# Attention taps by way of a DRAM buffer, bands by a masked multiply, and the combine in source order

## The chip, the cores and the metric

The kernel runs on one core of a Trainium2 chip. The metric is the device time of one execution in microseconds (us), taken over several runs. A profiled execution of the kernel before the change gives the views that are quoted below.

## The reference

First a short convolution whose weights differ per token and head: 8 batches of 3584 tokens with 192 features, 8 heads of 24 features, 7 taps. The taps of each token and head are softmaxed. Then a soft mixture of experts over all 28672 tokens with 32 slots and 8 experts.

```python
w = exp(weight_gen - max over taps); w = w / (sum over taps + 1e-09)
out[b, s, h*24:(h+1)*24] = sum over k of w[b, s, h, k] * x_pad[b, s + k, h*24:(h+1)*24]   # x_pad: 6 zero rows in front
logits = out @ phi                                   # 28672 x 32
d = softmax of logits over the tokens;  slot_input = d.T @ out
slot_out[e] = relu(slot_input[e] @ w1[e]) @ w2[e]
result = (softmax of logits over the slots) @ slot_out
```

## The kernel before

**Tiling.** A block is 26 tokens (`T`). Four blocks make a group of 104 tokens, and there are 35 groups in a batch, 280 in all. TensorE works on two groups at a time, a *pair*, so there are 140 pairs. Eight pairs make a *unit* `u`. Seven groups, which are 3.5 pairs, make a *supergroup* `s`; there are 40 of them, and x and the taps are loaded by supergroup.

**The convolution as a matrix product.** For each block, and each half of the heads, a weight matrix is needed that has 4 bands on its partitions: 32 input rows for each of 4 heads, and 26 columns for the block's tokens. Column j holds the 7 taps of token j at rows j to j+6 and zero elsewhere. `conv` multiplies it with a block-diagonal tile of x (`xbd`, two buffers) into one of three PSUM tiles (`cvs`), and ScalarE copies the result to `tms`. A supergroup has 56 such bands (`NBC`).

**How a band is made before.** The host lays the taps out by token with 8 slots (`KS`), tap k of token j at slot (j+k) mod 8. `loadw` brings one supergroup. `taps_top` (VectorE) finds the maximum, `taps_exp` subtracts it (VectorE) and takes the exponential (ScalarE), `taps_sum` sums and inverts (VectorE), `taps_norm` multiplies (GpSimd). `bandw` then makes half a supergroup's bands: `band_mult` (GpSimd) repeats the 8 slots four times and multiplies by the band mask, with tokens on partitions, and `band_turn` (VectorE) transposes 32x32 blocks so that the input rows come onto the partitions.

**What follows.** `xpose` transposes `tms` on TensorE and ScalarE copies it to `cms`. Once per unit: `logits` (TensorE, then maximum `mx` and `mq` on VectorE), `dexp` (the matmul `pm`, then an exponential), `dturn` and `save` (VectorE transposes), `dispatch` (TensorE) and `rescale` (VectorE). `soft_step` walks through the softmax over slots, half a batch at a time, on VectorE, GpSimd and ScalarE. After the last unit come the experts, and then the combine: for each piece of the output `rows` multiplies on TensorE, `leave` copies from PSUM on ScalarE and VectorE in turn and sends the piece to DRAM, and `turn` (VectorE) transposes the softmaxed logits of a later batch into `cT`.

**What sets the order.** A planner with its own estimate of times orders the instructions of PE, DVE, ACT and POOL, except inside blocks that are marked `manual_schedule`, where program order holds: the start (DVE, POOL, ACT) and the stretch from the last unit to the end of the experts (all four). SP, which issues every DMA, always follows program order: an issue that waits holds up all that stand behind it. `loadx(s)` waits until `conv` has finished with supergroup s-2. In the loop, `loadw(s+3)` stands at the start of supergroup s, behind `loadx(s+1)`.

## Time and profile before

| what | value |
|---|---|
| median of 3 runs | 400.87 us (398.52 to 402.51) |
| profiled execution | 401.48 us, of which the span of its instructions is 399.8 us |
| busy share of the span | PE 80%, DVE 78%, POOL 64%, ACT 47% |
| DMA | 72.69 MB, mean 182 GB/s |
| mean granted TensorE clock | 0.897 of full |

Shares are of the whole span, which has stages with different limits: a start of some 22 us, the loop over units until about 310 us, the experts until 331 us, and the combine, in which the output is written. An engine's busy time includes time in which an instruction has begun and is held by another engine. "DVE idle before, released by DMA" means that an instruction of VectorE waited for a transfer.

### The profile page before, as it was taken

The numbers are of one execution on the slowest core, as the hardware profiler recorded it, in microseconds if no ns is written. First come the engines' busy times: TensorE is split into PE (matmuls) and PEld (weight loads), VectorE is DVE, ScalarE is ACT, GpSimd is POOL, SyncE is SP. The second block draws the span as 40 slices with busy tenths as digits, with TensorE's granted clock in tenths as the row PEclk, the third lists the DMA queues.
The fourth block names the chain that finished last, engine by engine and source line by source line (L and its number), as shares of the span: only waits on it lengthen the run. The fifth ranks groups of instructions, "written<-read, shape, count | busy, mean of one in ns | idle before, by whom it ended". The sixth has DMA issues, their size and how long they took to land.

```text
span 399.8 us, 15122 instructions
## 1 busy us (share of the span) xinstructions
PE 318.3 (80%) x6624; PEld 225.8 (56%) x6624; DVE 313.8 (78%) x494; ACT 189.4 (47%) x409; POOL 257.1 (64%) x203
## 2 busy tenths in 40 slices
PE   7867777869788797986978889875889894999940
PEld 7656556647466685764757676664667651323310
DVE  8999697896899979998888978899695559654430
ACT  7555453546365564554545446563555112443320
POOL 7887777977689899598967797798694430000000
PEclk9999998998999989989897989999899999595555
DMA  6554965864763643646433375543447901999996
GB/s 179 153 142 118 271 199 150 236 203 143 212 178 96 167 114 93 168 117 158 107 106 99 95 176 132 131 119 93 117 117 285 349 5 48 362 397 399 399 402 235
DMA packets 22866, 72.69 MB, mean 182 GB/s; under 512 B 4241, under 2 KB 9489, under 8 KB 22289
## 3 DMA queue, kind: packets, MB, share of 16 engines
q1 hardware_dynamic: 22800, 71.73, 58.5%
q8 instruction: 52, 0.85, 1.0%
q14 instruction: 14, 0.11, 0.1%
HBM read 49.35 MB, written 22.36 MB: 179 GB/s over the span
## 4 chain that ended last, share of the span: by engine, by line
DVE 40%; PE 21%; DMA 18%; SPq 11%; issue 4%; ACT 2%; POOL 1%; ACTq 0%; DVEq 0%; POOLq 0%
DMA wbuf<-wh 16%; DVE wbuf L231 12%; PE cv L255 8%; SPq L651 6%; DVE en L198 5%; SPq L183 5%; DVE wmx L193 4%; DVE wsm L205 3%; DVE mq L300 3%; PE pt L268 3%; PE po L642 3%; DVE wsm L206 2%; DMA out<-big 2%; DVE mx L298 2%; DVE sm L76 1%
## 5 line engine op out<-in xcount | busy, mean ns | idle before, releaser
L215 POOL TENSOR_TENSOR wbuf<-en,mask 128x896 f32<-128x896 f32 (+1 forms) x83 | 170.6, 2076 | 5.5 <-DVE en L211 3.0
L255 PE MATMUL cv<-big,wbuf 128*26 128x96 f32 x4480 | 139.0, 259 | 31.2 <-DVE wbuf L231 20.3
L255 PEld LDWEIGHTS cv<-big,wbuf 128*26 128x26 f32 x4480 | 107.8, 110 | 53.7 <-DVE wbuf L231 27.3
L258 ACT COPY tm<-cv 128x384 f32<-128x384 f32 x140 | 65.9, 481 | 62.8 <-PE cv L255 57.8
L231 DVE STREAM_TRANSPOSE wbuf<-wbuf 128x896 f32<-128x896 f32 (+1 forms) x84 | 87.3, 1043 | 1.7 <-POOL wbuf L215 1.6
L268 PE MATMUL pt<-ident,tm 122*128 122x122 f32 x420 | 75.3, 296 | 6.5 <-ACT tm L258 5.8
L270 ACT COPY cm<-pt 128x312 f32<-128x312 f32 x139 | 56.9, 422 | 31.1 <-PE pt L268 30.4
L211 POOL TENSOR_TENSOR en<-en,wsm 128x448 f32<-128x448 f32 (+1 forms) x38 | 36.8, 967 | 40.8 <-DVE wsm L206 27.3
L268 PEld LDWEIGHTS pt<-ident,tm 122*128 122x128 f32 x420 | 46.1, 148 | 28.4 <-ACT tm L258 8.7
L642 PE MATMUL po<-cT,so 32*128 32x468 f32 (+3 forms) x256 | 47.4, 853 | 6.4 <-DVE big L649 5.4
L193 DVE TENSOR_REDUCE wmx<-wbuf 128x56 f32<-128x448 f32 (+1 forms) x41 | 24.0, 587 | 26.2 <-DMA wbuf<-wh 26.2
L649 DVE COPY big<-po 128x936 f32<-128x936 f32 (+1 forms) x24 | 26.2, 1102 | 22.0 <-DMA out<-big 11.7
L198 DVE TENSOR_TENSOR en<-wbuf,wmx 128x448 f32<-128x448 f32 (+1 forms) x40 | 43.1, 1078 | 0.1
L649 ACT COPY big<-po 128x936 f32<-128x936 f32 (+1 forms) x24 | 21.9, 918 | 39.1 <-PE po L642 20.1
L200 ACT ACTIVATE en<-en 128x448 f32<-128x448 f32 (+1 forms) x41 | 23.4, 573 | 33.3 <-DVE en L198 31.2
L642 PEld LDWEIGHTS po<-cT,so 32*128 32x128 f32 (+1 forms) x256 | 15.7, 217 | 37.0 <-ACT big L649 19.5
L205 DVE TENSOR_REDUCE wsm<-en 128x56 f32<-128x504 f32 (+1 forms) x41 | 26.6, 649 | 6.1 <-ACT en L200 6.1
L294 PE MATMUL ls<-cm,phi_sb 128*32 128x208 f32 (+1 forms) x576 | 30.2, 334 | 0.7 <-ACT al L330 0.7
L349 PE MATMUL ac<-tm,dt 128*32 128x193 f32 x544 | 27.6, 329 | 0.0
L79 POOL TENSOR_TENSOR LT<-LT,sm 128x576 f32<-128x576 f32 (+1 forms) x16 | 18.6, 1163 | 8.1 <-DVE sm L77 7.9
L294 PEld LDWEIGHTS ls<-cm,phi_sb 128*32 128x32 f32 x576 | 20.5, 109 | 4.4 <-ACT al L330 0.9
L313 PE MATMUL pm<-mq,sel 128*128 128x5 f32 (+1 forms) x36 | 6.6, 255 | 19.2 <-DVE mq L300 18.8
(106 smaller groups left out, 274.1 us busy)
## 6 DMA issues: line engine op xcount, KB each, us to landing
big<-xh SPq DMA_DIRECT2D x160, 168.0 KB, 3.4
out<-big SPq DMA_DIRECT2D x24, 468.0 KB, 6.7
out<-big SPq DMA_DIRECT2D x24, 442.0 KB, 6.8
wbuf<-wh SPq DMA_DIRECT2D x40, 224.0 KB, 3.8
big<-w SPq DMA_DIRECT2D x7, 768.0 KB, 7.5
w1a_sb<-w1a SPq DMA_DIRECT2D x4, 1024.0 KB, 6.7
w1b_sb<-w1b SPq DMA_DIRECT2D x4, 512.0 KB, 9.3
wbuf<-w SPq DMA_DIRECT2D x1, 768.0 KB, 11.3
```

Source lines behind the costliest of these rows:

```text
L193: V.tensor_reduce(out=mx[:, :, 0], in_=wgs[s][:, lo : lo + n], axis=AX.X, op=ALU.max)
L198: i = eng.tensor_tensor(out=en, in0=wgs[s][:, lo : lo + n], in1=mx.to_broadcast([128, n, KS]), op=ALU.subtract)
L205: V.tensor_reduce(out=sm[:, :, 0], in_=ens[s % NEN][:, lo : lo + n], axis=AX.X, op=ALU.add)
L215: eng.tensor_tensor(out=wt[:, lo : lo + n].rearrange("p b (a q) -> p b a q", q=KS), in0=wn.rearrange("p b (o q) -> p b o q", o=1) .to_broa ...
L231: turns.append(V.transpose(w[:, lo : lo + n].rearrange("p b i -> p (b i)"), wt[:, lo : lo + n].rearrange("p b i -> p (b i)")))
L255: P.matmul(cv[32 * blk : 32 * blk + T, o : o + 96], Ws[s, bc // (NBC // 2)][:, bc % (NBC // 2), 0:T], xb[:, :, bc * GW : (bc + 1) * GW], s ...
L258: A.copy(tms[u % NTM][:, pr, 1 : 2 * D + 1], cv[:, 0 : 2 * D])
L268: P.transpose(pt[:, i, 0:TR], tm[0:TR, pr, 1 + 128 * i : 129 + 128 * i], ident[0:TR, 0:TR])
L270: copy(cms[u][:, pr].rearrange("p i b j -> p (i b) j"), pt.rearrange("p i (b j) -> p (i b) j", j=32)[:, :, 0:T])
L294: P.matmul(lp[32 * blk : 32 * blk + 32, 0:n, par, 0:T], phi_sb[:, 2 * par + i, :], cm[:, 0:n, 1 if i else 2 * par, blk, :], start=(i == 0) ...
L642: P.matmul(po[dst : dst + hi - lo, q % 2, 0 : n * T], so[32 * q : 32 * q + 32, lo:hi], cT[32 * q : 32 * q + 32, g0 : g0 + n, 0:T], start=T ...
L649: (V.tensor_copy if done[1] % 2 else A.copy)(ot.rearrange("p (q c) -> p q c", q=2), po[:, :, 0 : n * T])
```

## The change

The supergroups 0 and 1 keep the old way, in buffers that lie in `w1a_sb` until the experts' weights arrive. The other 38 are taken two at a time, as 19 *chunks*. In a chunk the seven taps lie in seven planes of L = 112 elements. VectorE finds the maximum and the sum with a tree of three two-input operations over the planes, GpSimd subtracts and normalizes, ScalarE takes the exponential. `send` writes the normalized taps to a DRAM buffer with eight DMAs, each taking every eighth partition, so that tap k of token j lands at row j+k, slot j mod 8, in runs of 448 bytes. `fetch` reads the buffer back by row, so that the input rows are on the partitions. `reslot` (ScalarE) copies the slots to be innermost, and `band_make` (VectorE) repeats them along the 26 columns and multiplies by the transposed mask. GpSimd's `band_mult` and VectorE's `band_turn` fall away for these supergroups.

The issue order on SP changes with it: per chunk one load of taps instead of two, eight sends, one fetch, and the eight loads of x as before. The two DRAM buffers are zeroed at the start. The combine runs in program order on DVE, ACT and PE, and the last expert's second matrix gets a buffer of its own.

```diff
+CG = 14
+L = 2 * NBC
+NCH = B * NG // CG
...
+    NXB, NTM, NCV, NRAW, NBAND, NSLOT = 2, 2, 3, 3, 3, 1
...
+    early = w1a_sb.rearrange("p e f -> p (e f)")
...
+    raws = [fix.tile([128, KS, L], F32, name=f"raw{i}") for i in range(NRAW)]
+    rows8 = [fix.tile([128, KS, L], F32, name=f"rows{i}") for i in range(2)]
+    slots = [fix.tile([128, L, KS], F32, name=f"slots{i}") for i in range(NSLOT)]
+    bands = [fix.tile([128, NBC, T], F32, name=f"band{i}") for i in range(NBAND)]
+    via = [dram.tile([128 + KS, KS, L], F32, name=f"via{i}") for i in range(2)]
...
+    def loadw(ch):
+        SY.dma_start(raws[ch % NRAW][:, 0:KT], wh[ch - 1])
+    def chunk_exp(ch, eng=G):
+        raw = raws[ch % NRAW]
+        t = pa.tile([128, 4, L], F32, tag="tree", name=f"top{ch}")
+        V.tensor_tensor(out=t, in0=raw[:, 0:4], in1=raw[:, 3:KT], op=ALU.max)
+        V.tensor_tensor(out=t[:, 0:2], in0=t[:, 0:2], in1=t[:, 2:4], op=ALU.max)
+        V.tensor_tensor(out=t[:, 0], in0=t[:, 0], in1=t[:, 1], op=ALU.max)
+        w = raw[:, 0:KT]
+        i = eng.tensor_tensor(out=w, in0=w, in1=t[:, 0:1].to_broadcast([128, KT, L]),
+                              op=ALU.subtract)
+        A.activation(w, w, AF.Exp)
+        return i
+    def chunk_sum(ch):
+        raw = raws[ch % NRAW]
+        t = pa.tile([128, 4, L], F32, tag="tree", name=f"sum{ch}")
+        V.tensor_tensor(out=t, in0=raw[:, 0:4], in1=raw[:, 4:KS], op=ALU.add)
+        V.tensor_tensor(out=t[:, 0:2], in0=t[:, 0:2], in1=t[:, 2:4], op=ALU.add)
+        V.tensor_tensor(out=t[:, 0], in0=t[:, 0], in1=t[:, 1], op=ALU.add)
+        V.reciprocal(t[:, 0], t[:, 0])
+        return t
+    def chunk_norm(ch, t, eng=G):
+        w = raws[ch % NRAW][:, 0:KT]
+        eng.tensor_tensor(out=w, in0=w, in1=t[:, 0:1].to_broadcast([128, KT, L]), op=ALU.mult)
+    def send(ch):
+        for q in range(KS):
+            SY.dma_start(via[ch % 2][q : q + 128].rearrange("(m k) s l -> m k s l", k=KS)
+                         [:, 0:KT, q], raws[ch % NRAW][q::KS, 0:KT])
+    def fetch(ch):
+        SY.dma_start(rows8[ch % 2], via[ch % 2][0:128])
+    def reslot(ch):
+        A.copy(slots[ch % NSLOT], rows8[ch % 2].rearrange("p q b -> p b q"))
+    def band_make(s):
+        r = slots[s // 2 % NSLOT][:, s % 2 * NBC : (s % 2 + 1) * NBC]
+        w = bands[s % NBAND]
+        a = T // KS
+        V.tensor_tensor(out=w[:, :, 0 : a * KS].rearrange("p b (a q) -> p b a q", q=KS),
+                        in0=r.rearrange("p b (o q) -> p b o q", o=1)
+                        .to_broadcast([128, NBC, a, KS]),
+                        in1=maskT[:, :, 0 : a * KS].rearrange("p o (a q) -> p o a q", q=KS)
+                        .to_broadcast([128, NBC, a, KS]), op=ALU.mult)
+        V.tensor_tensor(out=w[:, :, a * KS : T], in0=r[:, :, 0 : T % KS],
+                        in1=maskT[:, :, a * KS : T].to_broadcast([128, NBC, T % KS]), op=ALU.mult)
...
                     P.matmul(cv[32 * blk : 32 * blk + T, o : o + 96],
-                             Ws[s, bc // (NBC // 2)][:, bc % (NBC // 2), 0:T],
+                             Ws[s, bc // HB][:, bc % HB, 0:T] if s < 2 else
+                             bands[s % NBAND][:, bc],
...
-    loadw(0)
+    loadw0(0)
+    loadw0(1)
+    loadx(0)
     loadw(1)
-    loadx(0)
     SY.dma_start(phi_sb, phi)
-    loadw(2)
+    for t in via:
+        SY.dma_start(t[0:128], rows8[0])
...
     conv(0, 0)
     sm = taps_sum(1)
...
-    mx = taps_top(2)
+    chunk_exp(1, V)
     band_turn(w, wt, 0, QB)
...
-    taps_exp(mx, 2)
+    t = chunk_sum(1)
+    chunk_norm(1, t, V)
+    send(1)
     band_turn(w, wt, 0, QB)
     conv(0, 2)
...
+    fetch(1)
+    loadx(2)
+    chunk_exp(2)
     conv(0, 4)
...
+    rs2 = chunk_sum(2)
...
     start.close()
+    chunk_norm(2, rs2)
+    send(2)
+    reslot(1)
+    band_make(2)
+    conv(0, 6)
+    xpose(0, 5)
+    loadx(3)
+    fetch(2)
+    band_make(3)
+    loadw(4)
+    chunk_exp(3)
+    conv(0, 7)
...
+            ch, i = divmod(p0 + pr, CG // 2)
+            if i == 0 and ch + 3 < NCH:
+                loadw(ch + 3)
+            if i == 0 and 2 < ch + 2 < NCH:
+                chunk_exp(ch + 2)
+            if i == 1 and 2 < ch + 2 < NCH:
+                chunk_norm(ch + 2, chunk_sum(ch + 2))
+            if i == 3 and ch + 2 < NCH:
+                send(ch + 2)
+            if i in (3, 6) and 2 * ch + 2 + i // 6 < NSG:
+                loadx(2 * ch + 2 + i // 6)
...
+            if i == 6 and ch + 2 < NCH:
+                fetch(ch + 2)
+            if i == 1 and ch + 1 < NCH:
+                reslot(ch + 1)
+            if i in (2, 4) and ch + 1 < NCH:
+                band_make(2 * ch + 2 + i // 4)
...
-    w2l = wpart(0, WE)
+    w2l = pc.tile([128, WE], F32, name="w2l", bufs=1)
...
+    ctx.enter_context(tc.manual_schedule(engines={
+        mybir.EngineType.DVE, mybir.EngineType.Activation, mybir.EngineType.PE}))
     for kind, b, st in out_order():
```

120 lines of the change are left out of this document (44 added, 76 removed).

## The prediction

> **What bounds the kernel now.** I read the engines' shares by stage first, then TensorE's waits in the longest stage, then the chain that ended last, then single instructions. The windows give time, then busy time and count for PE, weight loads, DVE, ACT and POOL, then the granted clock, the DMA share and GB/s:
>
> ```profile
> span 399.8 us, 15122 instructions
> ...
> 36.00:310.00 274.00, 225.37 (x5472) 175.39 (x5472) 234.50 (x364) 142.30 (x335) 219.89 (x164) 0.94 0.55 152
> ...
> 331.00:340.00 9.00, 3.66 (x24) 1.32 (x24) 9.00 (x15) 2.68 (x3) 0.00 (x0) 0.90 0.13 53
> 340.00:400.00 60.00, 43.71 (x232) 14.38 (x232) 25.15 (x24) 19.25 (x21) 0.00 (x0) 0.59 0.93 365
> ```
>
> The loop (36 to 310) takes 274 us, and PE is busy for 225.4 of them: 48.6 us of idle time is all that a better supply of bands can win there. DVE has 234.5 and POOL 219.9, so no engine is full; they wait for each other. From 340 on DMA is at 0.93 with 365 GB/s: the output is bound by the transfer, and what can be won there is an earlier beginning. PE's waits inside the loop, and the chain over the whole span:
>
> ```profile
> PE cv L255 <- DVE wbuf L231: 19.5, 17, 3.2
> PE pm L313 <- DVE mq L300: 16.7, 10, 3.8
> PE cv L255 <- issue: 5.4, 3, 2.7
> ...
> DVE wmx L193 <- DMA wbuf<-wh: 26.2, 16, 3.5
> ...
> DMA wbuf<-wh 16%; DVE wbuf L231 12%; PE cv L255 8%; SPq L651 6%; DVE en L198 5%; SPq L183 5%; DVE wmx L193 4%; DVE wsm L205 3%; DVE mq L300 3%; PE pt L268 3%; PE po L642 3%; DVE wsm L206 2%; DMA out<-big 2%; DVE mx L298 2%; DVE sm L76 1%
> ```
>
> The reader sees a ring: conv ends, SP gets past the loads of x, the next taps are loaded, DVE and POOL make bands, the next conv starts. 16% of the chain is the transfer of the taps, DVE waits 26.2 us for it, and PE waits 19.5 us for the transpose that ends each band. The second wait is for mq, a tiny instruction that DVE reaches late.
>
> **The change on DVE.** The old way, per supergroup, and the short forms that give a price per element:
>
> ```profile
> L231 DVE STREAM_TRANSPOSE wbuf<-wbuf 128x896 f32<-128x896 f32 x76 | 82.6, 1088 | 1.7 <-POOL wbuf L215 1.6
> L198 DVE TENSOR_TENSOR en<-wbuf,wmx 128x448 f32<-128x448 f32 x38 | 41.8, 1099 | 0.1
> L205 DVE TENSOR_REDUCE wsm<-en 128x56 f32<-128x504 f32 x39 | 25.8, 661 | 6.1 <-ACT en L200 6.1
> L193 DVE TENSOR_REDUCE wmx<-wbuf 128x56 f32<-128x448 f32 x39 | 23.3, 598 | 26.2 <-DMA wbuf<-wh 26.2
> L206 DVE RECIPROCAL wsm<-wsm 128x56 f32<-128x56 f32 x39 | 18.7, 481 | 0.1
> L211 DVE TENSOR_TENSOR en<-en,wsm 128x224 f32<-128x224 f32 x3 | 1.0, 373 | 0.0
> L206 DVE RECIPROCAL wsm<-wsm 128x28 f32<-128x28 f32 x2 | 0.7, 328 | 0.1
> L215 DVE TENSOR_TENSOR wbuf<-en,mask 128x448 f32<-128x448 f32 x1 | 0.6, 624 | 0.0
> ```
>
> Removed per chunk (two supergroups): 2 x (0.598 + 1.099 + 0.661 + 0.481 + 2 x 1.088) = 10.03 us. Added: a two-input operation takes 0.624 us for 448 elements and 0.373 for 224, so 1.12 ns each, which gives 0.25 us for 112, 1.00 for 784 and 1.63 for 1344. Two trees of 448, 224 and 112 cost 2.49. The reciprocal grows by (0.481 - 0.328)/28 = 5.5 ns an element, 0.79 for 112. Two bands at 1.63 + 0.25 cost 3.76. Together 7.04.
>
> That is without POOL in the way. The same 448 elements take 0.624 us once and 1.099 on average at L198: 0.475 us is lost while POOL is busy 219.9/274 = 80% of the time.
>
> ```profile
> L198 DVE TENSOR_TENSOR en<-wbuf,wmx x40: 393/888/2323, 3.9 to 291.5; 128x448 f32<-128x448 f32 x38, 128x224 f32<-128x224 f32 x2
> L215 POOL TENSOR_TENSOR wbuf<-en,mask 128x896 f32<-128x896 f32 x70 | 149.0, 2149 | 2.3 <-DVE wbuf L231 0.5
> L211 POOL TENSOR_TENSOR en<-en,wsm 128x448 f32<-128x448 f32 x35 | 34.2, 978 | 39.4 <-DVE wsm L206 25.9 <-DVE nm L315 6.2 <-DVE mq L300 4.8
> ```
>
> Its longest, 2.32 us, exceeds the short form by 1.7 us, most of one POOL instruction (2.15). The loop holds 35 supergroups, 17.5 chunks (35 norms at L211). POOL loses 149.0 + 34.2 = 183.2 us there and keeps 36.7, 2.1 per chunk; subtract and norm of 784 elements at 978/448 = 2.18 ns add 3.42. 5.5 us in some 14.5 is 38%. So each of the ten two-input instructions of a chunk loses 0.475 x 38/80 = 0.23 us, 2.3 together; the bounds are 0 and all of POOL's 5.5. DVE comes to 9.3 per chunk, against 10.03. **DVE therefore wins only 0.7 x 17.5 = 12 us of work**; the gain must come from when the work can be done, since the taps of a chunk are now loaded a whole chunk ahead of their first use.
>
> The Trainium skill, SBUF — State Buffer, section Who interferes with whom, says that a VectorE instruction with two SBUF inputs and a GpSimd instruction that reads SBUF shut each other out, the second waiting until the first is done. By that rule the upper bound, 5.5 us per chunk, is what the ten instructions could meet at worst; L198's spread agrees with it.
>
> **ACT.** Two exponentials of 448 (0.582) become one of 784, and the slot copy comes new:
>
> ```profile
> L200 ACT ACTIVATE en<-en 128x448 f32<-128x448 f32 x39 | 22.7, 582 | 32.0 <-DVE en L198 29.9 <-DVE nm L315 1.6 <-POOL dd L320 0.4
> L649 ACT COPY big<-po 128x936 f32<-128x936 f32 x12 | 11.3, 939 | 26.2 <-PE po L642 16.2 <-DMA out<-big 8.7 <-DVE big L649 1.4
> L372 ACT COPY big<-zero 128x1344 f32<-128x1344 f32 x3 | 3.7, 1302 | 0.0
> ```
>
> The exponential comes to about 0.87 (582 x 784/448 less a fixed part), the copy of 896 to 0.90 by the 936 row. Its input steps 448 bytes, which no row shows; I bound it by 0.90 and the 1.30 of the 1344 row and take 0.90. ACT gains 0.6 per chunk and stays at 142 + 11 of some 254 us: free, as long as the copy is not put where its fetch has not landed.
>
> **DMA and SP.**
>
> ```profile
> DMA packets 22866, 72.69 MB, mean 182 GB/s; under 512 B 4241, under 2 KB 9489, under 8 KB 22289
> ...
> q1 hardware_dynamic: 22800, 71.73, 58.5%
> ...
> big<-xh SPq DMA_DIRECT2D x160, 168.0 KB, 3.4
> ...
> 143.82 1.70 SPq L183 DMA_DIRECT2D big<-xh  x4
> 145.62 0.37 SPq L188 DMA_DIRECT2D wbuf<-wh  x1
> ```
>
> A chunk adds 8 sends of 16 x 7 runs of 448 bytes (0.40 MB in 896 packets) and a fetch of 0.46 MB; the loads of taps fall from 0.46 to 0.40 MB. In the loop 152 GB/s took a share of 0.55, so 276 GB/s at full share: 0.80 MB more are 2.9 us per chunk. By packets it is far more: 58.5% of 16 engines over 399.8 us for 22800 packets is 0.164 us each, 896 x 0.164/16 = 9.2 us for the sends alone. The loop now uses 0.55 x 274/17.5 = 8.6 per chunk. I take the bytes, 11.5 of 14.5, because a run is a seventh of the mean packet (3.2 KB); the other end, about 19.5, would bind. The Trainium skill, DMA: Bandwidth & Descriptors, section Specifications, puts the least run for full rate at 512 bytes, with a read-modify-write below; no run here has a packet of 448 bytes, and by that rule the sum would move toward the packet end.
>
> SP issues one DMA in 0.37 to 0.43 us, so 18 instead of 10 per chunk are some 7.3 us of its 14.5. Behind each send, which waits for POOL's norm, stands loadx(2ch+2).
>
> **The start loses.** Rows of PE, DVE and SP:
>
> ```profile
> 10.22 0.64 DVE L205 TENSOR_REDUCE wsm<-en 128x56 f32<-128x504 f32 x1
> ...
> 12.47 0.86 PE L255 MATMUL cv<-big,wbuf 128*26 128x96 f32 x30 [0.44 <-DVE wbuf L231]
> 16.93 1.51 PE L255 MATMUL cv<-big,wbuf 128*26 128x96 f32 x60 [0.16 <-DVE wbuf L231]
> 22.24 0.95 PE L255 MATMUL cv<-big,wbuf 128*26 128x96 f32 x36
> ```
>
> Pair 7, the first that needs supergroup 2, starts at 22.24. After: the sum of supergroup 1 ends near 11.9 (memsets add 0.4). Three maxima and a subtraction of 784 take 1.25 + 1.00 plus some 0.4 behind POOL, to 14.5, ahead of the turns that pair 1 waits for. Two turns and two norms (1.9), the second tree and reciprocal with POOL's four band_mults beside them (2.6), and the norm (1.8 with its wait) reach 20.7. Eight sends take 3.4 to issue and land near 27, the fetch takes about 4 (the x row's 3.4 and more bytes) to 31, the copy 1, the band 1.9: pair 7 starts at 34. PE has run dry from 28 on. **+12 us**, with 8 and 15 as bounds (each of the two transfers 2 us shorter or 1.5 longer). Zeroing the DRAM buffers, 0.92 MB, lies under this.
>
> **The loop wins.** The bands are made from taps loaded 14 us earlier, so the 19.5 us wait for L231 goes: -19.5. The mq wait is half DVE's queue and half POOL's lock; with POOL at half its load I take half, -8. New waits come in: of 38 loads, 16 found DVE waiting, 26.2 us, which is 0.69 per load. Of the 17.5 fetches, reads by ACT, and loads of x behind sends, I charge 0.43 us each, as three PSUM tiles stand between ACT and PE: +7.5 (bounds 0 and 17.5 x 26.2/16 = 29). Sum -20, a loop of 254 us. Check: DVE would be at (234.5 - 12)/254 = 0.88, against 0.86 now; PE at 225.4/254 = 0.89.
>
> **The combine wins.**
>
> ```profile
> 331.19 7.82 DVE L450 STREAM_TRANSPOSE cT<-LT 128x576 f32<-128x576 f32 x12
> 338.94 3.12 DVE L649 COPY big<-po 128x936 f32<-128x936 f32 x3
> ...
> out<-big SPq DMA_DIRECT2D x24, 468.0 KB, 6.7
> ```
>
> The planner put twelve turns, 7.82 us, ahead of DVE's first output copy at 338.94; the 331 to 340 window moves 53 GB/s. In program order the copy comes first and a turn (0.65) follows two pieces, of which DVE copies one (1.1): 1.8 per two pieces, under the 2 x 0.47 MB/400 GB/s = 2.3 of their transfer. The output can flow from about 334 instead of 340: **-6 us** (bounds -3 and -7).
>
> Sum against the profiled execution: 401.5 + 12 - 20 - 6 = 387.5. The profiled time is 0.6 above the median 400.87, so I say **387**.
>
> **Rivals.** *All waits go.* Bands and mq both vanish and nothing new comes, so that PE stands idle 8 us of the loop instead of 48.6: -40, and 401.5 + 12 - 40 - 6 = 367. For it: supply far ahead. Against it: DVE would need 222 of 234 us, 95%.
>
> *SP's queue holds x.* From the start of a chunk's tree to the end of its norm: 1.25 + 1.71 + 0.87 + 2.04 + 1.71 = 7.6 us (tree, subtract, exponential, sum with reciprocal, norm), and 3.4 for the sends, before loadx(2ch+2) can go. x has 3.5 pairs, some 7 us, of which its issue (1.7) and landing (3.4) take 5, so 2 are spare. If DVE starts the tree no earlier than its place in the source, x comes 11.0 - 7 - 2 = 2 us late in each chunk: +35 in place of the +7.5, and 401.5 + 12 - 27.5 + 35 - 6 = 415. It decides as soon as the norm ends after conv(2ch). Against it: the taps are there early, and DVE may run ahead by the third band buffer.
>
> *The loop does not move*, because DVE stays as late as it was (2.3 us of lock grow to 4): 401.5 + 12 - 6 = 407. For it: DVE's work is nearly the same.
>
> *Packets bind.* At the packet end a chunk's DMA takes 19.5 against 274/17.5 = 15.7 now: +67, 475; at 0.1 us a packet 5.6 + 1.7 + 8.6 = 15.9, about 411.
>
> **How the numbers follow.** Forecast 0.43 (380 to 397), all waits go 0.17, SP's queue 0.20, no move 0.13, packets 0.07. The runs lie 1% apart, so 1% (4 us) is what a measurement can tell from no change. Faster: the forecast nearly whole and the 367 case, 0.59. Within 1%: the forecast's edge and part of "no move", 0.08. Slower 0.33. Low 370 leaves out a part of the best case; high 415 leaves out the packets and half of SP's queue.
>
> **What would show it.** Right: pair 7 near 34 with PE idle ahead of it; no PE wait of size on DVE bands in the loop; loop PE share near 0.89; output at full rate from 334. Wrong: SP waiting on POOL's norm with x late behind it, ACT's slot copy waiting on the fetch for over 1 us per chunk, band multiplies far over 1.9 us, or a DMA share near 1 in the loop.

## The result and the profile after

| | before | after |
|---|---|---|
| median of 4 runs each, same chip | 401.69 us (398.52 to 409.45) | 437.69 us (435.65 to 441.35) |
| profiled execution, its span | 401.48, 399.8 us | 435.69, 434.0 us |
| ratio after/before, 95% interval | | 1.0935 [1.0806, 1.1064] |

The changed kernel is 9.35% slower. The forecast was 387 us, with a range from 370 to 415 us: the time went the other way, and lies above the range. Some executions run a few per cent slower throughout; ratios compare undisturbed ones, and the traces of five runs (the two without sends and fetches, one send, four sends behind each x, sends and fetches on GpSimd's queue) are of disturbed ones, from which prices and waits are read, not times.

First the stages, from the windows of the changed kernel (time, then busy time and count of PE, weight loads, DVE, ACT and POOL, then granted clock, DMA share and GB/s):

```profile
span 434.0 us, 15304 instructions
...
36.00:347.00 311.00, 248.90 (x5699) 190.67 (x5688) 191.23 (x342) 172.52 (x343) 100.92 (x91) 0.90 0.65 179
...
371.00:434.00 63.00, 45.37 (x256) 15.78 (x256) 34.00 (x37) 21.83 (x24) 0.00 (x0) 0.67 0.91 356
```

POOL and DVE have far less to do than before, and the loop is longer all the same. Marks in the trace split the difference of the spans: the conv of pair 7 begins at 22.24 before and 35.48 after, the experts' first matmul at 316.06 and 356.0, the combine's first at 331.33 and 371.28. So the start costs 13.2 us, **the loop 26.7 us (293.8 to 320.5)**, experts nothing, and the combine wins 5.8 (68.5 to 62.7). The same stretch, pair 7 to experts, in the windows of the kernel before and then of the kernel after:

```profile
22.00:316.00 294.00, 240.61 (x5842) 187.17 (x5841) 251.34 (x386) 150.76 (x358) 233.07 (x176) 0.95 0.56 155
```

```profile
35.00:356.00 321.00, 257.30 (x5839) 196.85 (x5840) 197.22 (x357) 176.09 (x353) 103.04 (x97) 0.90 0.66 185
```

The reader sees two parts in the 27 us. PE's idle time grows from 53.4 to 63.7 us, where the forecast had it shrink by 20. And PE's busy time for the same matmuls grows by 16.7 us, at a granted clock of 0.90 instead of 0.95. DVE's busy time falls by 54 us and buys nothing.

PE's waits over the whole span of the changed kernel (line, releaser: us in total, times, longest):

```profile
PE cv L314 <- DMA big<-xh: 28.4, 16, 3.7
PE pt L328 <- ACT tm L318: 15.2, 11, 5.0
PE pt L328 <- ACT cm L330: 5.9, 7, 1.6
PE pm L373 <- DVE mq L360: 5.7, 7, 1.9
PE cv L314 <- DVE w1a_sb L295: 5.2, 2, 3.0
PE ac L409 <- DVE dt L394: 4.7, 4, 1.7
```

The wait for bands is gone, and the wait for mq fell from 16.7 to 5.7. In their place PE waits 28.4 us for x, which did not appear among its waits before, and 21 us for ScalarE (6 before). In the loop alone (36 to 347) the waits for x, `tm`, `cm` and `dt` are 48.5 us. x is not carried more slowly: it lands 3.8 us after its issue, against 3.4 before.

```profile
big<-xh SPq DMA_DIRECT2D x160, 168.0 KB, 3.8
```

It is issued late, and SP shows why. Its waits in the loop of the changed kernel:

```profile
SPq L236 <- POOL raw L231: 54.2, 12, 7.2
SPq L199 <- PE cv L314: 22.0, 14, 7.5
```

A piece of its timeline there (start, length, then the issues in a row):

```profile
199.41 5.15 SPq L236 DMA_DIRECT2D via<-raw  x8
204.66 6.18 SPq L199 DMA_DIRECT2D big<-xh  x8
210.94 0.37 SPq L240 DMA_DIRECT2D rows<-via  x1
211.41 0.38 SPq L205 DMA_DIRECT2D raw<-wh  x1
216.97 6.02 SPq L236 DMA_DIRECT2D via<-raw  x8
```

Before, SP was ahead of the work. In the loop (36 to 310) it waited for the conv at each x:

```profile
SPq L183 <- PE cv L255: 166.9, 33, 9.7
```

Now it waits 54.2 us for GpSimd's normalization, then needs 6.0 us for eight sends (the median of the loop's 17 rows, 5.2 to 8.8), and only then comes x, here both supergroups' in one row. The sends by themselves in the changed kernel (min/median/max in ns):

```profile
L236 SPq DMA_DIRECT2D via<-raw x152: 532/597/2043, 21.3 to 316.3; - x152
```

From its groups of instructions (busy us and mean ns, then the idle time before them) the band multiply, the slot copy and the norm:

```profile
L250 DVE TENSOR_TENSOR band<-slots,maskT 128x1344 f32<-128x1344 f32 x38 | 60.4, 1590 | 50.5 <-ACT slots L243 50.3
L243 ACT COPY slots<-rows 128x896 f32<-128x896 f32 x19 | 33.3, 1751 | 28.9 <-DMA rows<-via 28.8
L231 POOL TENSOR_TENSOR raw<-raw,sum 128x784 f32<-128x784 f32 x18 | 33.4, 1856 | 42.5 <-DVE sum L226 33.7
```

The chain that ended last now begins with the way through DRAM, and SP has three places on it:

```profile
DMA rows<-via 11%; PE cv L314 9%; SPq L236 8%; DMA out<-big 6%; SPq L199 5%; DMA big<-xh 5%; PE pt L328 4%; DMA raw<-wh 4%; ACT slots L243 4%; DVE band L250 3%; POOL raw L231 2%; POOL raw L215 2%; SPq L716 2%; PE ls L354 2%; DMA via<-raw 1%
```

### The profile page after: what moved, and what is told of

Read it like the earlier page. It is cut to its first block, busy times and chain, and to the rows that moved or that the text cites. A ratio compares the mean times of both kernels' runs of the same rounds, so it can differ in the third digit from the quotient of the medians.

```text
span 434.0 us, 15304 instructions
## 1 busy us (share of the span) xinstructions
PE 337.7 (78%) x6624; PEld 239.1 (55%) x6624; DVE 266.3 (61%) x480; ACT 218.1 (50%) x410; POOL 130.1 (30%) x127
## 4 chain that ended last, share of the span: by engine, by line
DMA 27%; PE 20%; DVE 18%; SPq 16%; ACT 7%; POOL 5%; issue 4%; ACTq 0%; DVEq 0%; POOLq 0%
DMA rows<-via 11%; PE cv L314 9%; SPq L236 8%; DMA out<-big 6%; SPq L199 5%; DMA big<-xh 5%; PE pt L328 4%; DMA raw<-wh 4%; ACT slots L243 4%; DVE band L250 3%; POOL raw L231 2%; POOL raw L215 2%; SPq L716 2%; PE ls L354 2%; DMA via<-raw 1%
## 5 line engine op out<-in xcount | busy, mean ns | idle before, releaser
L314 PE MATMUL cv<-big,band 128*26 128x96 f32 x4256 | 137.7, 274 | 34.1 <-DMA big<-xh 28.4
L314 PEld LDWEIGHTS cv<-big,band 128*26 128x26 f32 x4256 | 111.4, 117 | 53.7 <-issue 42.4
L318 ACT COPY tm<-cv 128x384 f32<-128x384 f32 x140 | 65.8, 484 | 54.4 <-PE cv L314 53.4
L250 DVE TENSOR_TENSOR band<-slots,maskT 128x1344 f32<-128x1344 f32 x38 | 60.4, 1590 | 50.5 <-ACT slots L243 50.3
L215 POOL TENSOR_TENSOR raw<-raw,top 128x784 f32<-128x784 f32 x18 | 34.6, 1920 | 101.9 <-DVE top L213 62.9
L243 ACT COPY slots<-rows 128x896 f32<-128x896 f32 x19 | 33.3, 1751 | 28.9 <-DMA rows<-via 28.8
L707 PE MATMUL po<-cT,so 32*128 32x442 f32 (+3 forms) x256 | 45.4, 771 | 2.0 <-DVE big L714 0.7
L231 POOL TENSOR_TENSOR raw<-raw,sum 128x784 f32<-128x784 f32 x18 | 33.4, 1856 | 42.5 <-DVE sum L226 33.7
L714 DVE COPY big<-po 128x936 f32<-128x936 f32 (+1 forms) x24 | 26.2, 1097 | 16.3 <-DMA out<-big 9.5
L707 PEld LDWEIGHTS po<-cT,so 32*128 32x128 f32 (+1 forms) x256 | 15.8, 199 | 30.5 <-ACT big L714 14.5
L409 PEld LDWEIGHTS ac<-tm,dt 128*32 128x32 f32 x544 | 18.8, 119 | 14.2 <-DVE dt L394 5.6
L217 ACT ACTIVATE raw<-raw 128x784 f32<-128x784 f32 x19 | 16.3, 857 | 18.6 <-POOL raw L215 13.6
L74 POOL TENSOR_TENSOR LT<-LT,rm 128x576 f32<-128x576 f32 (+1 forms) x16 | 18.9, 1185 | 18.9 <-DVE rm L72 18.9
```

Of the source, the lines that this page charges most:

```text
L215: i = eng.tensor_tensor(out=w, in0=w, in1=t[:, 0:1].to_broadcast([128, KT, L]), op=ALU.subtract)
L231: eng.tensor_tensor(out=w, in0=w, in1=t[:, 0:1].to_broadcast([128, KT, L]), op=ALU.mult)
L243: A.copy(slots[ch % NSLOT], rows8[ch % 2].rearrange("p q b -> p b q"))
L250: V.tensor_tensor(out=w[:, :, 0 : a * KS].rearrange("p b (a q) -> p b a q", q=KS), in0=r.rearrange("p b (o q) -> p b o q", o=1) .to_broadc ...
L314: P.matmul(cv[32 * blk : 32 * blk + T, o : o + 96], Ws[s, bc // HB][:, bc % HB, 0:T] if s < 2 else bands[s % NBAND][:, bc], xb[:, :, bc * ...
L318: A.copy(tms[u % NTM][:, pr, 1 : 2 * D + 1], cv[:, 0 : 2 * D])
```

## The experiments

Three theories were on record. **A**: SP's order and its time, since the sends wait for the normalization, take long to issue, and hold x. **B**: ScalarE's slot copy, 1.75 us where it was priced 0.90. **C**: the added transfers, 16 MB and nearly 20,000 packets. All ratios are to the kernel before, run beside each kernel on its chip.

**x ahead of the sends.**

```diff
+            if i in (3, 6) and 2 * ch + 2 + i // 6 < NSG:
+                loadx(2 * ch + 2 + i // 6)
             if i == 3 and ch + 2 < NCH:
                 send(ch + 2)
-            if i in (3, 6) and 2 * ch + 2 + i // 6 < NSG:
-                loadx(2 * ch + 2 + i // 6)
```

> The changed kernel with one edit: in the loop the loads of x for supergroup 2ch+2 are issued on SP ahead of the eight sends instead of behind them. Theory A (SP's queue: the sends wait for GpSimd's norm and hold x back, PE waits 28.4 us for x): the wait of conv for x falls to under 10 us and the time falls by 15 to 25 us, to 412 to 422. Theory B (ScalarE: the slot copy of 1.75 us and its wait for the fetch hold back the copies that TensorE needs): within 5 us of the changed kernel's 437. Theory C (the added DMA traffic makes every transfer late): within 5 us, and x still lands late after its issue.

1.0396 [1.0314, 1.0478]: 5.4 points come back, nearly what A forecast in time. But PE's wait for x did not fall below 10 us as A said, it rose to 35.5 us, and x landed 4.9 us after its issue instead of 3.8. The sends (5.9 to 7.1 us in a row) now stand ahead of the other x of the chunk. So the order matters, but this one only moves the sends ahead of another load.

**Sends on GpSimd's queue, and sends and fetches there.** In the second run the `fetch` of the loop goes to `G` too.

```diff
-            SY.dma_start(via[ch % 2][q : q + 128].rearrange("(m k) s l -> m k s l", k=KS)
+            eng.dma_start(via[ch % 2][q : q + 128].rearrange("(m k) s l -> m k s l", k=KS)
...
-                send(ch + 2)
+                send(ch + 2, G)
```

> The changed kernel with the loop's sends issued from GpSimd's queue, right behind its norm, instead of SP's. Theory A: SP no longer waits for the norm at all, so x and the fetches go on time; -15 to -30 us if GpSimd issues eight sends in under 8 us per chunk, and worse than 437 if an issue there costs well over 1 us. Theory B: the wait of ScalarE for the fetch stays, within 8 us of 437. Theory C: no change.

> The changed kernel with the loop's sends and fetches issued from GpSimd's queue; SP issues x and the taps alone. With the sends alone there, SP waited 147 us for them in front of the fetch and x stood behind that fetch. Theory A: with the fetch moved too, x stands behind nothing but conv and the taps, its wait falls to under 8 us, and the kernel gets faster by 15 to 30 us, 407 to 422, unless GpSimd's wait for the sends to land delays its subtract and norm (then 430 or more, with VectorE waiting for the slots). Theory B and C: no change.

1.0934 [1.0867, 1.1001] and 1.1187 [1.1044, 1.133]. SP's wait in the first run:

```profile
SPq L240 <- DMA via<-raw: 147.0, 53, 16.7
```

The fetch, still on SP, now waits for the sends to land and holds x in the same way: PE waits 23.7 us for it. With the fetch moved too, x is no longer among PE's largest waits, as A said, but `dt` (28.1 us) and bands (24.8 us) are, and the time is longer still. To move the issues to GpSimd is no cure.

**The loop's x on ScalarE's queue.**

```diff
-                loadx(2 * ch + 2 + i // 6)
+                loadx(2 * ch + 2 + i // 6, A)      # ScalarE issues it instead of SP
```

> The changed kernel with the loop's loads of x issued from ScalarE's queue, so that they stand behind no send and no fetch; ScalarE has copied the last result of that supergroup anyway. It pays about 8 x 0.42 us of issue per chunk. Theory A: TensorE's wait for x falls to under 8 us, -15 to -30 us if ScalarE (173 of 311 us busy in the loop) has room for the issues: 407 to 422. Theory B: ScalarE is what binds, so 3.4 us more per chunk on it make the kernel slower, 440 to 470. Theory C: no change.

1.112 [1.1018, 1.1223]. PE's waits:

```profile
PE cv L314 <- DVE band L255: 34.7, 10, 9.0
PE pt L328 <- ACT cm L330: 16.0, 7, 6.2
...
PE cv L314 <- DMA big<-xh: 3.9, 2, 2.0
```

The wait for x fell to 3.9 us, but bands and `cm` took its place: an issue that waits for the conv now stands in ScalarE's order, ahead of the slot copy and the evictions. A queue that is already in order for other work is no free place.

**The sends left out.**

```diff
-        for q in range(KS):
+        for q in range(0):
             SY.dma_start(via[ch % 2][q : q + 128]...
```

> The changed kernel with the sends left out: the fetch reads the zeroed DRAM buffer, so the bands of 38 supergroups are zero; norm, fetch, slot copy and band multiplies stay. SP then neither waits for GpSimd's norm nor spends 6 us per chunk on issuing eight sends. Theory A (SP's queue holds x): TensorE's 28 us of waiting for x fall to under 10 and the time falls by 20 to 35 us, to 402 to 417. Theory B (ScalarE's slot copy): the copy keeps its 1.75 us, -5 to -10. Theory C (DMA traffic): 6.8 of 88.9 MB go, 17024 of 42610 packets; x lands in about the 3.8 us of before anyway, so at most -5.

1.0295 [1.0189, 1.0401], with a wait for x of 7.1 us. So 6.4 of the 9.35 points hang on the sends; whether by issue, wait or bytes this run can't say, though C had allowed 5 us at most and it is some 20 us.

**Copy in storage order, and no copy at all.** In the first, ScalarE's copy reads the fetched rows as they lie; in the second, the band multiplies read them with the step of 448 bytes.

```diff
-        A.copy(slots[ch % NSLOT], rows8[ch % 2].rearrange("p q b -> p b q"))
+        A.copy(slots[ch % NSLOT].rearrange("p b q -> p (b q)"), rows8[ch % 2].rearrange("p q b -> p (q b)"))
...
-        r = slots[s // 2 % NSLOT][:, s % 2 * NBC : (s % 2 + 1) * NBC]
+        r = rows8[s // 2 % 2][:, :, s % 2 * NBC : (s % 2 + 1) * NBC].rearrange("p q b -> p b q")
```

> The changed kernel with ScalarE's slot copy flat: 896 elements in storage order, without putting the slots innermost, so the bands hold the wrong taps. If the step of 448 bytes is what makes the copy 1.75 us, it falls to about 0.90 us as the 936-element row has it; if it stays near 1.75, something else (two SBUF sides) does. Theory B: 0.85 x 19 = 16 us less on ScalarE, time -5 to -16. Theory A: the ring through SP gets 0.85 us shorter per chunk, x still late, 0 to -6.

> The changed kernel without the slot copy: the band multiplies read the fetched rows directly, stepping 448 bytes from slot to slot. Theory B: ScalarE loses 33 us of copies and its 26 us of waiting for the fetch, PE's waits on ScalarE (9.5 + 5.9 us in the loop) go, -12 to -25 us. Theory A: the ring through SP gets shorter by the 1.75 us copy per chunk, at most -10. On the price of the stride: if VectorE pays for it as ScalarE does (1.75 against 0.90), the band multiply goes from 1.59 to about 3 us and the gain is eaten up (+0 to +20).

1.0722 [1.0616, 1.0827] and 1.1126 [1.1062, 1.119]. The copy of the first, then the band multiply of the second:

```profile
L243 ACT COPY slots<-rows 128x896 f32<-128x896 f32 x19 | 17.9, 940 | 23.1 <-DMA rows<-via 23.1
```

```profile
L249 DVE TENSOR_TENSOR band<-rows,maskT 128x1344 f32<-128x1344 f32 x38 | 99.5, 2618 | 37.5 <-DMA rows<-via 37.4
```

The step costs ScalarE 1.751 against 0.940 us and VectorE 2.618 against 1.590. The Trainium skill, SBUF — State Buffer, section Door 1: The DMA port swizzle, says that accesses which cross to a new 16-byte line each time pay a penalty; both rows agree. By the ratios B is worth about 2 points, not 9; the two intervals touch, and the medians (437.69 and 434.02 us) lie under 1% apart, so it may be less.

**The loop without sends and fetches, and without the copies too** (the second run takes away all six lines).

```diff
-            if i == 3 and ch + 2 < NCH:
-                send(ch + 2)
...
-            if i == 6 and ch + 2 < NCH:
-                fetch(ch + 2)
-            if i == 1 and ch + 1 < NCH:
-                reslot(ch + 1)
```

> The changed kernel with the loop's sends and fetches left out (the start's stay): from supergroup 6 on the bands are made from rows fetched once, so these supergroups take wrong taps; ScalarE's copy, VectorE's bands and all arithmetic stay. Leaving out the sends alone gave 1.030 of the kernel before, with 300 us from pair 7 to the experts where the kernel before has 294. A (SP's order): with the sends gone SP is already free, so the fetches cost nothing more: 1.02 to 1.035. B (ScalarE's copy, 1.76 us where it was priced 0.90, sits between evictions that TensorE waits for): the copy stays and no longer waits for rows, 1.01 to 1.03. C (added DMA traffic): the last of it is gone, 0.97 to 1.00, as the prediction had for the loop.

> As the run without sends and fetches, and the loop's copies on ScalarE are left out too (bands from supergroup 4 on are made from the first chunk's slots, wrong taps). What is left of the change in the loop is VectorE's and GpSimd's cheaper work. A: no change against the run with the copies, within 0.01. B: 18 copies of 1.76 us leave ScalarE, the loop falls to the forecast's 274 us and the time to 0.96 to 0.98 of the kernel before. C: 0.97 to 1.00, as without fetches.

1.0151 [0.9999, 1.0303] and 1.0045 [0.9975, 1.0116]. With nothing left of the way through DRAM in the second loop, and DVE and POOL relieved, the kernel should have been at the forecast's 0.96, and by its sum without the new waits (401.5 + 12 - 27.5 - 6 = 380) at 0.95. It is no faster than before; B, at 0.96 to 0.98, missed too. **Some four points of the forecast's gain never existed**, whatever the sends do.

**The same with the taps loaded three pairs earlier.** VectorE waited 26.1 us for taps in the run just told. A fourth theory, **D**, is that the taps arrive late because their load stands behind x on SP.

```diff
-            if i == 0 and ch + 3 < NCH:
-                loadw(ch + 3)
+            if i == 4 and ch + 4 < NCH:
+                loadw(ch + 4)
```

> The changed kernel without the loop's sends, fetches and slot copies (wrong taps from supergroup 4 on, as in the run before it that measured 1.0045), and with each chunk's taps loaded three pairs earlier (at step 4 of the chunk before instead of step 0). D (taps late behind x on SP): VectorE's wait for raw falls from 26 us to under 8, TensorE's wait for mq from 24 us to under 12, and the time to 0.965 to 0.985 of the kernel before. Rival (the loop is bound by TensorE's own 251 us and its clock, whoever waits): no change, 1.00 to 1.01.

1.0077 [1.0007, 1.0146]: no change. VectorE's wait for the taps stayed at 25.2 us, so the edit did not remove what it was to remove, and D is not decided by it. Its loop in the windows:

```profile
36.00:321.00 285.00, 246.01 (x5840) 189.63 (x5840) 214.84 (x356) 144.31 (x333) 115.53 (x97) 0.94 0.54 157
```

PE's largest waits in it:

```profile
PE pm L373 <- DVE mq L360: 22.5, 10, 4.2
PE cv L314 <- DMA big<-xh: 5.7, 4, 2.2
```

PE's idle time fell from 53.4 to 39.0 us: 14 of the forecast's 20. Its busy time rose by 5.4, and mq, which the forecast had at 8.7, stands at 22.5. In this run the band's wait is gone and the wait for mq has grown.

**Constant sends in the kernel before**, ahead of an x and behind it.

```diff
                 if i == 3 and s + 2 < NSG:
+                    if s % 2 == 0 and s + 4 < NSG:
+                        send(s // 2)      # 8 x 49 KB of a constant tile, no engine to wait for
                     loadx(s + 2)
```

> The kernel before, with eight sends of 49 KB of a constant to DRAM (the same 16x7 runs of 448 bytes) put ahead of the x of every even supergroup of the loop, where the changed kernel has its sends; they wait for no engine. A in its first form (the cost is SP's wait for GpSimd's normalization): 1.00 to 1.01, since nothing waits. A in a second form (the eight issues themselves, 8 x 0.6 us, come ahead of an x that has 8.2 us per supergroup for its 1.7 us of issue and 3.8 us to landing, 2.7 us to spare): x late by 2 to 3 us once in 16 us, 1.03 to 1.08, and TensorE waits for x by 20 us or more. B: 1.00. C: 1.02 to 1.05, by traffic, with x landing later than 3.8 us.

> As the last one, with the eight constant sends behind that x instead of ahead of it. A in both forms: 1.00 to 1.02, TensorE waits for x by less than 8 us. B: 1.00. C: the same traffic, so the same time as with the sends ahead.

1.0131 [1.0016, 1.0246] and 1.0323 [1.0193, 1.0453]. Ahead of the x, A's second form missed: it had expected at least 1.03 and 20 us of waiting for x. Behind it both forms of A missed (1.02 at most), and C, which had expected the same time in both. PE's waits in the loop for bands and for x, with the sends ahead and then behind:

```profile
PE cv L264 <- DVE wbuf L240: 11.0, 11, 2.2
PE cv L264 <- DMA big<-xh: 9.2, 6, 2.7
```

```profile
PE cv L264 <- DVE wbuf L240: 19.4, 21, 2.3
PE cv L264 <- DMA big<-xh: 10.8, 3, 4.8
```

So in the kernel before, eight sends that wait for nothing cost one to three points, not nine. That they cost more behind the x is clear (411.68 to 417.5 us against 404.09 to 408.92). There the next thing on SP is the load of taps, but the wait for bands was 19.5 us without any sends too, so the reason is not shown.

**All tap steps most of a chunk earlier.** Load, subtraction, exponential, sum and normalization move ahead by three to five pairs; the sends stand behind the x of step 6, the fetch at step 2. Of the edit, the new lines without those for the first chunk:

```diff
+            if i == 4 and ch + 4 < NCH:
+                loadw(ch + 4)
+            if i == 2 and ch + 3 < NCH:
+                chunk_exp(ch + 3)
+            if i == 3 and ch + 3 < NCH:
+                chunk_norm(ch + 3, chunk_sum(ch + 3))
+            if i == 2 and 3 < ch + 2 < NCH:
+                fetch(ch + 2)
             if i in (3, 6) and 2 * ch + 2 + i // 6 < NSG:
                 loadx(2 * ch + 2 + i // 6)
+            if i == 6 and ch + 3 < NCH:
+                send(ch + 3)
```

> The changed kernel, complete, with the tap steps of a chunk moved ahead: load at step 4 instead of 7 (of the chunk three before), subtraction and exp five pairs earlier, normalization five, the eight sends four pairs earlier and behind the x of step 6, the fetch four pairs earlier. Lateness (A in its wider form): SP's wait for the normalization falls from 54 us to under 10, VectorE's wait for slots from 41 us to under 10, TensorE's wait for x to under 12, and the time to 1.01 to 1.035 of the kernel before. Transfers and issues (C): 17 MB more and 160 more issues stay, 1.05 or more, with x landing later than 3.8 us and waits for x of 20 us or more.

1.0921 [1.075, 1.1091]: no gain. SP's wait for the normalization did fall, from 54.2 to 13.3 us; VectorE's wait for slots only to 31.3. But PE's largest wait, and then two of SP's, were:

```profile
PE cv L314 <- DMA big<-xh: 44.7, 14, 9.2
```

```profile
SPq L240 <- DMA via<-raw: 25.1, 22, 2.8
SPq L236 <- POOL raw L231: 13.3, 4, 7.7
```

The fetch now stands ahead of an x and waits for the sends to land. So taking away the wait for GpSimd alone gains nothing: with that nearly gone, x is later than ever. It also landed 5.0 us after its issue, as C had said. The lateness theory in this form fell, and what was left was SP's own time or the transfers.

**One send instead of eight.** The same 392 KB and the same 448-byte runs, in one transfer. The slots land rotated, so this kernel leaves out what would put them right.

```diff
-        for q in range(KS):
-            SY.dma_start(via[ch % 2][q : q + 128].rearrange("(m k) s l -> m k s l", k=KS)
-                         [:, 0:KT, q], raws[ch % NRAW][q::KS, 0:KT])
+        v = via[ch % 2][0:128]
+        to = bass.AP(tensor=v.tensor, offset=v.offset,
+                     ap=[[KS * L, 128], [KS * L + L, KT], [1, L]])
+        SY.dma_start(to, raws[ch % NRAW][:, 0:KT])
```

> The changed kernel with the eight sends of a chunk merged into one transfer of the same 448-byte runs and the same 392 KB, to rows and slots that a single pattern can reach (the slots land rotated: wrong taps; fetch, copy and bands as they are). SP's time for the sends falls from 5 to 6.5 us per chunk to under 1 us, packets and bytes stay. SP's time as the cause: TensorE's wait for x falls from 48 us to under 15, the time to 1.03 to 1.05 of the kernel before, near the run without sends (1.030). Transfers as the cause: 1.07 to 1.10.

**1.0074 [1.0001, 1.0147]**: 8.6 of the 9.35 points are gone, more than either theory had expected. Its issues of the send:

```profile
L238 SPq DMA_DIRECT2D via<-raw x19: 377/377/389, 21.3 to 286.7; - x19
```

PE's and then SP's waits in its loop:

```profile
PE pt L329 <- ACT cm L331: 13.9, 11, 3.9
...
PE cv L315 <- DMA big<-xh: 6.0, 5, 3.1
```

```profile
SPq L238 <- POOL raw L231: 84.4, 17, 7.6
SPq L199 <- PE cv L315: 74.8, 21, 7.4
```

Its packets, and the time from issue to landing of the taps' load and the send:

```profile
DMA packets 40481, 88.86 MB, mean 218 GB/s; under 512 B 21600, under 2 KB 21984, under 8 KB 39904
...
raw<-wh SPq DMA_DIRECT2D x19, 392.0 KB, 6.2
via<-raw SPq DMA_DIRECT2D x19, 392.0 KB, 3.9
```

SP waits for the normalization even longer, 84.4 us, but at x it waits for the conv again, 74.8 us instead of 22.0, and PE's wait for x is 6.0 us. x still lands after 3.9 us. The bytes are the same 88.9 MB, the small packets fewer by a tenth only. So neither the wait for GpSimd by itself nor the bytes hold the loop: that the send is eight transfers in a row does. C, against the loop with nothing of the way through DRAM (1.0045), is worth about a point at most. Of A its second form is left, the time of the row. In the kernel before the same row cost far less (1.0131 and 1.0323); there SP stood waiting for the conv 166.9 us of the loop, and here the row begins only when a late normalization ends. That the two together make up the difference is argued, not shown.

**Four sends behind each x, the kernel complete.** Tap steps ahead as above, sends 0 to 3 behind the x of step 6, 4 to 7 behind that of step 3, the fetch behind the x of step 6. Of the edit, the lines for sends and fetch:

```diff
             if i in (3, 6) and 2 * ch + 2 + i // 6 < NSG:
                 loadx(2 * ch + 2 + i // 6)
+            if i == 3 and 3 < ch + 2 < NCH:
+                send(ch + 2, KS // 2, KS)
+            if i == 6 and ch + 2 < NCH:
+                fetch(ch + 2)
+            if i == 6 and ch + 3 < NCH:
+                send(ch + 3, 0, KS // 2)
```

> The changed kernel, complete, with the tap steps ahead as in the run with lead, but four of a chunk's sends behind each x (0 to 3 at step 6, 4 to 7 at step 3 of the next chunk), and the fetch behind the x of step 6: between two x SP now has 1.7 + 2.9 us of issues and no wait for a landing, against 8.2 us per supergroup. SP's time as the cause: TensorE's wait for x under 10 us, 1.01 to 1.04. Transfers as the cause: 1.06 or more, with x landing later than 4.5 us.

1.0415 [1.0332, 1.0497], just above A's range. The wait for x was 9.0 us, as expected of A, but another 8.9 us of the conv's wait is put down to the sends' landing. x landed after 3.8 us, against C. This one leaves nothing out and is 5.2 points below the changed kernel by order and lead alone.

**The combine's order alone, in the kernel before**, then its taps loaded a supergroup earlier by a fourth buffer, then both.

```diff
+    ctx.enter_context(tc.manual_schedule(engines={
+        mybir.EngineType.DVE, mybir.EngineType.Activation, mybir.EngineType.PE}))
     for kind, b, st in out_order():
...
-    NWB, NWT, NWG = 4, 2, 3
+    NWB, NWT, NWG = 4, 2, 4
...
-                    if s + 3 < NSG:
-                        loadw(s + 3)
+                    if s + 4 < NSG:
+                        loadw(s + 4)
```

> The kernel before with one part of the change alone: the combine in program order on DVE, ACT and PE. The combine of the changed kernel took 62.7 us from its first multiply to the end of the span, against 68.5 before, so -5.7 us is expected: 395 to 396. If the gain in the changed kernel came from elsewhere (TensorE's clock, the matrix in its own buffer), no change: 401.

> The kernel before with a fourth buffer of taps, so that each supergroup's taps are loaded one supergroup (8.2 us) earlier. D: VectorE's wait for the taps falls from 26 us to under 5, TensorE's waits for the band and for mq (19.5 and 16.7 us) fall by a third or more, 0.97 to 0.99. Rival: VectorE waits where it would have had to wait for POOL and TensorE anyway, 0.995 to 1.005.

> As the last one, and the combine's copies and turns in program order on VectorE, ScalarE and TensorE, which alone gave 0.9835 of the kernel before. If the two add: 0.955 to 0.975 under D, 0.98 to 0.985 under its rival.

0.9835 [0.9783, 0.9887], 0.9952 [0.9892, 1.0012] and 0.9833 [0.9746, 0.992]. The order wins 1.65%, some 6.6 us, and is the part of the change that pays. Taps earlier win nothing clear of the noise, alone or with the order. But VectorE's wait for the taps fell only from 26.2 to 17.3 us, not below 5, so this does not decide D either. No version of this study is faster than the kernel before with the combine in order.

## Why the prediction was wrong, step by step

**The start: right.** Forecast +12 with pair 7 at 34; it was +13.2 at 35.48. The timeline of PE in the changed kernel, then that of SP:

```profile
34.09 0.87 PE L328 MATMUL pt<-ident,tm 122*128 122x122 f32 x3 [5.00 <-ACT tm L318]
35.48 2.77 PE L314 MATMUL cv<-big,band 128*26 128x96 f32 x72 [0.53 <-DVE band L255]
```

```profile
21.27 5.49 SPq L236 DMA_DIRECT2D via<-raw  x8
28.21 0.34 SPq L240 DMA_DIRECT2D rows<-via  x1
```

The sum through the norm (20.7; they began at 21.27) was good. The eight sends took 5.49 us and not 3.4, and this row already held the price that decided the loop. The slot copy was 0.7 us longer than forecast too (1.71 for 1). A shorter landing paid part of both back: from the last send's issue at 26.76 to the fetch at 28.21 it took 1.5 us, where the forecast had 2.9. So the sum came out partly because its errors cancelled.

**The combine: right.** Forecast -6, measured -5.8. DVE's copies and turns alternate in the changed kernel, and the output flows at 356 GB/s over the whole stage (371 to 434):

```profile
372.50 1.13 DVE L714 COPY big<-po 128x936 f32<-128x936 f32 x1 [1.27 <-PE po L707]
373.55 0.77 DVE L516 STREAM_TRANSPOSE cT<-LT 128x576 f32<-128x576 f32 x1
374.24 1.04 DVE L714 COPY big<-po 128x884 f32<-128x884 f32 x1
```

**DVE's work: prices right, the lock too dear.** The band multiply was forecast at 1.63 and took 1.590. The rows add up to 7.6 us a chunk (two trees, a reciprocal, two bands), where 7.04 and 2.3 of loss to POOL were forecast, so the loss hardly came, and DVE's busy time fell by 54 us from pair 7 to the experts instead of 12. It changed nothing that can be seen in the time.

**The slot copy: mis-sized.** 0.90 was taken, bounds to 1.30, and it is 1.751. The prediction saw that no row had such a step and bounded it by two rows without a step, so neither bound could hold it. By the flat copy it is worth 2 points at most; with one send the copy is as long (1.733 us in the median) and the whole loss is 0.7 points, so these points do not simply add.

**The band and mq: right, then undone.** -19.5 and -8 were forecast; the waits went from 19.5 to near nothing and 16.7 to 5.7. But where the sends are gone, mq is back at 22.5: these waits are not terms that can be taken away one by one. PE waits for what comes last, and when one is removed the next one shows. So the -27.5 was too much by itself: with the way through DRAM gone from the loop, PE's idle time fell by 14 us.

**The new waits, +7.5 with bounds 0 and 29: this step failed.** PE's waits for x, tm, cm and dt came to 48.5 us in the loop, 28.4 of them for x. The +7.5 is 0.43 us once a chunk, for fetches, reads by ScalarE and x together. Its price was taken from the old loads of taps, which stood behind four issues of x, while x now stood behind eight sends. The prediction priced a send by other DMAs' 0.37 to 0.43 us and added them to SP's load on average, "7.3 us of its 14.5". What counts is the row of issues ahead of one x: eight at 0.6 us, 5.2 to 8.8 with their waits, against the 2 us that x had to spare by the prediction's own rival.

**The rival "SP's queue holds x"** (415 us, 0.20) named the place. It took the wait for the norm as what decides and 3.4 us for the sends. Its sign, SP waiting on POOL's norm with x late behind it, was seen. The runs turn the rest round: with the norm's wait cut to 13.3 us nothing was won, and with one issue instead of eight almost all was, at 84.4 us of that wait. "Packets bind" fell: the loop's DMA share is 0.65. From pair 7 to the experts 155 GB/s took a share of 0.56 before and 185 took 0.66 after, which is 277 and 280 GB/s at full share, so the prediction was right to count bytes (276). The Trainium skill, DMA: Bandwidth & Descriptors, section Specifications, puts the least run for full rate at 512 bytes; the runs of 448 bytes showed no such loss, since these two figures agree. (An estimate: at half the rate the loop's sends, 6.8 MB, would have taken 24 us more, 0.08 of the share.)

**PE's busy time was taken as fixed, 225.4 of the loop.** It was not: 257.3 against 240.6 us from pair 7 to the experts, with the clock at 0.90 against 0.95. No term of the sum had it. The two traces show where it comes from. Their clock is granted in full or in half, in stretches of 3.4 us and multiples of it, and from pair 7 to the experts it is at half for 31 us before and for 64 us after. An estimate from these: 33 us more at half speed cost half of that, 16.5 us, close to the 16.7. In the 3.4 us ahead of each half-speed stretch that begins there (8 before, 15 after) PE was busy for 0.59 of the time or less; where the clock stayed full it was busy for 0.97 before and 0.94 after in the median, and 0.47 at the least. By this PE's waits are paid for twice: once as idle time, and once more in the slower matmuls behind them. The estimate is rough: the run with the tap steps ahead has 70 us at half clock and 253.4 us of busy time, less than the changed kernel. The Trainium skill, TensorE: Matmul & The Clock Gate, section What's actually happening, says that an idle window of about 3.4 us puts the array back to half clock; here no window had to be idle throughout, since the longest gap in any of these windows was 3.0 us. No run took the gaps away alone.

In sum, as an estimate: of the 50 us between forecast and measurement, some 35 (8.6 points) go when the eight transfers become one, with their share of the waits and of the half clock; the other 16 or so were never there to win, since with one send the loop is only some 4 us shorter (1.0074 x 401.5 - 401.5 - 13.2 + 5.8).

**What stays open.** The run without sends (1.0295) is slower than the one with one send, which does more; the planner orders both anew, and no run tells why. So one send, and not the absence of sends, is the cleaner comparison, and the 8.6 points carry that doubt. A row of sends is not issue alone: in the changed kernel's trace every transfer raises the same semaphore as the one eight issues before it, and sends wait for transfers that they do not touch (8.0 us for w1a in the loop; 56.2 us for x where ScalarE issued it). By the rows this is the smaller part: the shortest row of eight takes 5.15 us, and the mean of the loop's 17 is 6.3. The merged send takes away both. Why mq is late at 22.5 us in a kernel whose DVE has 25 us of waiting for taps is argued only: mq stands behind that wait in DVE's order.

## What to carry to other kernels

On a queue that issues in order, price a row of issues by what stands behind it: compare the whole row, with its waits, with the time that the next load has to spare, not with the queue's average load. Count transfers before bytes; one transfer of 896 runs took the queue 0.38 us, eight of 112 took it 6.0. And when a forecast takes a wait away, ask which wait is second: here 27 us of waits that were to go left a loop that was at best 4 to 9 us shorter. A wait of TensorE can cost more than itself, when the clock falls behind it.

## What the runs showed of the hardware that was not expected

- A transfer of 16 x 7 runs from every eighth partition takes 0.60 us to issue (median), one of 128 x 7 runs of the same length 0.377.
- TensorE's clock fell to half for 3.4 us or more behind windows in which it was busy for 0.59 or less (all 23 such stretches that begin in the two loops), though no gap within these windows was over 3.0 us. Some windows down to 0.47 were followed by full clock.
- A read with a step of 448 bytes costs ScalarE's copy a factor of 1.86 (1.751 to 0.940 us) and VectorE's multiply 1.65 (2.618 to 1.590), where only one of its two inputs has the step.
- Nearly 20,000 packets more, most of them of 448 bytes, raised the loop's DMA share from 0.56 to 0.66 only, and a single send of 392 KB landed in 3.9 us, sooner than the load of taps of the same size (6.2).
